# The last two chunks' output sums by Strassen in 128x256 products, behind all of h, with w_out's sums built by VectorE

## The chip, the cores and the metric

One core of a Trainium2 chip runs the whole program. The metric is the device time of one execution in microseconds (us). The runs shown are several executions of one program; the profile is of one more execution, with its own time beside it.

## The reference

Attention over 8 x 8 heads of 576 positions and 64 channels, with a window mask (half of the heads: the last 32 positions; the other half: every fourth of the last 128), gives x with 4608 tokens of 512 channels. A feed-forward block follows:

```python
scores = where(mask, 0.125 * q @ k.T, -1e9); attn = softmax(scores); x = attn @ v     # per head
h = x @ w_in                                    # 4608x512 by 512x2048
sp = np.maximum(h, 0.0) + np.log1p(np.exp(-np.abs(h)))        # softplus
g = h * erf(sp)
out = g @ w_out                                 # 4608x2048 by 2048x512
```

## The kernel before

Tokens go in nine chunks of 512 (`TOK`), d_ff in 16 blocks of 128 (`FT`), taken in 8 pairs (`SPC`, `PAIR`). Float32 values are kept as a high part, rounded to the type f32r, and a low part, so a product of two matrices is three TensorE products: high x high, high x low, low x high. Three chunks (`PAIRED`) are done plainly beside the attention. The other six form three pairs of chunks (`DOUBLES`), and h of a pair is computed by Strassen's scheme with seven products (`ORDER`, `mm1_big`): the two halves of the d_model contraction, the two blocks of a d_ff pair and the two chunks are the 2x2 blocks. A step d (0 to 23, 8 for each pair of chunks) has 7 x 6 = 42 products of 128x512. `take_big` adds the seven results into h of chunk A and chunk B of the pair; `load_left` fetches the left operands of step d + 2 from a DRAM buffer `ws` into one of two places in `win`.

Then `argument_big` makes softplus on ScalarE into `ls`, ScalarE makes erf of it in place, and `multiply_big` makes g = h * erf on VectorE. Chunk B's g goes to DRAM (`kept_g`), as its output sums come later; chunk A's is used at once.

The output sums (g @ w_out) are plain: an item is one pair of d_ff blocks of one chunk. `split_item` makes g's high and low part (`ghi` by ScalarE or VectorE, `glo` by VectorE), `products` are 2 x 4 x 3 = 24 products of 128x512 into four PSUM banks `acc`. `store` copies the four banks out when a chunk is done.

The order is written out by hand, and each engine runs its instructions in that order. `period(i)` runs item i of `ITEMS` in quarters of six products, and where `BIG` has i, the 42 products of a step of h in groups between the quarters. Steps 0 to 7 of h are in periods 0 to 7, steps 8 to 15 in 16 to 23, steps 16 to 23 in 32 to 39; the other periods have an item alone. There are 50 items; the last 16 are chunk 7 (A16 to A23) and chunk 8 (B16 to B23). In a period stand, in this order: the split of the item's second half; the first products of h and their takes; a quarter; products 2 and 3; erf of the step before; a quarter; `multiply_big` of A; the split of the next item's first half; products 4 and 5 with A's softplus; `multiply_big` of B; a quarter; product 6 with B's softplus; a quarter; transfers. `AFT` holds further jobs by period and quarter, above all the sums of the right operands of the next pair of chunks. The step's products alternate between two PSUM banks (`h` and `bank`, which is tile `tx`): product n waits until product n - 2 is taken. All loads and nearly all stores are issued by SyncE's queue (SP), in order.

PSUM has eight banks: `h`, `tx`, two for the attention (`sp`), four `acc`.

Of the kernel before, what the change touches and what calls it, by code (L numbers as in the profile page):

```python
# [29 lines left out]
DM, DF = 512, 2048  # L30
# [3 lines left out]
TOK = 512  # L34
NCH = NTOK // TOK
# [104 lines left out]
def attn_moe_kernel(ctx: ExitStack, tc: tile.TileContext, qk, v, masks, eye, w_in, w_out, out):  # L140
# [467 lines left out]
    def split(item, e, copy=None):  # L608
        ghi, glo = (work.tile([P, TOK], F32R, name=n) for n in ("ghi", "glo"))
        gs[item].append((ghi, glo))  # L610
        (copy or nc.vector.tensor_copy)(out=ghi, in_=e)  # L611
        nc.vector.tensor_tensor(out=glo, in0=e, in1=ghi.bitcast(F32), op=ALU.subtract)  # L612
# [22 lines left out]
    def mm(args):  # L635
        nc.tensor.matmul(args["out"], args["lhsT"], args["rhs"], start=args["start"], stop=args["stop"])  # L636
# [22 lines left out]
    def store(c):  # L659
        last = c == NCH - 1  # L660
        for tt in range(TOK // P):
            if c == 0:
                o = added[tt]
                nc.vector.tensor_tensor(out=o, in0=acc[tt], in1=o, op=ALU.add)
            else:
                if tt == 0 and c < PAIRED - 1:
                    o = doubles(2).bitcast(F32).rearrange("p n w -> p (n w)")[:, 0:DM]
                elif tt == 0:
                    o = small.tile([P, DM], F32, name="o", bufs=1)
                else:  # L670
                    o = io.tile([P, DM], F32, name="w", bufs=4)
                copy_for(tt)(out=o, in_=acc[tt])
            r = c * TOK + tt * P
            (nc.scalar if last and tt % 2 else nc.sync).dma_start(out=out[r:r + P, :], in_=o)
# [43 lines left out]
    def room_w():  # L718
        return [io.tile([P, TOK], F32, name="w", bufs=4) for _ in range(2)]
# [25 lines left out]
    for k in range(1, DOUBLES):  # L745
# [6 lines left out]
                    (i - 3, 3): [LESS["T4"], LO["T1"], HI["T4"], HI["B22"]],  # L752
                    (i - 2, 3): [LO["T4"], LO["B21"]], (i - 1, 3): [LO["B22"]]})

    def jobs(todo):
        for job, *args in todo:
            job(*args)

    ITEMS = [NT - 2, NT - 1] + [(kind_, i * SPC + k) for i in range(DOUBLES) for kind_ in "AB" for k in range(SPC)]

    def mm1_big(d, k):
        bank_ = (h, bank)[(7 * d + k) % 2]
        name = ORDER[k]
        w = left(NT + d).rearrange("p (b i c n) -> p b i c n", b=len(LEFT), i=2, c=2)[:, LEFT.index(name)]
        x = big[RIGHT[LEFT.index(name)]]
        for c in range(2):
            for n, (wi, xi) in enumerate(((0, 0), (0, 1), (1, 0))):
                nc.tensor.matmul(bank_, w[:, wi, c, :], x[c][:, xi, :],  # L768
                                 start=(c == 0 and n == 0), stop=(c == 1 and n == 2))

    def take_big(d, k):
        y = (h, bank)[(7 * d + k) % 2]
        if k == 0:
            hs["A", d], hs["B", d] = pair_of(d)
        a, b = hs["A", d], hs["B", d]
        add = lambda out, to: nc.vector.tensor_tensor(out=out, in0=y, in1=to, op=ALU.add)  # L776
        if k == 0:
            nc.vector.tensor_copy(out=a[:, 1], in_=y)  # L778
        elif k == 1:
            add(a[:, 0], a[:, 1])  # L780
        elif k == 2:
            add(b[:, 0], a[:, 1])
        elif k == 3:
            add(b[:, 1], b[:, 0])
        elif k == 4:
            add(a[:, 1], b[:, 1])
        elif k == 5:
            nc.vector.tensor_tensor(out=b, in0=y.rearrange("p (j n) -> p j n", j=1).broadcast_to([P, PAIR, TOK]),
                                    in1=b, op=ALU.add)
        else:  # L790
            add(b[:, 0], b[:, 0])

    def pair_of(d):
        if d % 2:
            return [work.tile([P, PAIR, TOK], F32, name="hc") for _ in range(2)]
        return [slab(i) for i in range(2)]

    def argument_big(kind_, d):
        if (kind_, d) in hs:
            ls[kind_, d] = work.tile([P, PAIR, TOK], F32, name="s")  # L800
            nc.scalar.activation(out=ls[kind_, d], in_=hs[kind_, d], func=AF.Softplus)  # L801

    def multiply_big(kind_, d):
        e = hs[kind_, d]
        nc.vector.tensor_tensor(out=e, in0=e, in1=ls[kind_, d], op=ALU.mult)
        gs[kind_, d] = []
        if kind_ == "B":
            nc.sync.dma_start(out=kept_g[d // SPC][d % SPC], in_=e)

    def load_g(item):  # L810
        kind_, d = item
        if kind_ == "B":
            e = work.tile([P, PAIR, TOK], F32, name="hc") if d % 4 > 1 else slab(1 - d % 4)
            nc.sync.dma_start(out=e, in_=kept_g[d // SPC][d % SPC])
            hs[item] = e

    def split_item(item, j):
# [3 lines left out]
    def item_products(item):  # L821
        if isinstance(item, int):
            _, ftp, run = STEPS[item]
            first, last = ftp == RUNS[run][1], ends(item)
        else:
            ftp = item[1] % SPC
            first, last = ftp == 0, ftp == SPC - 1
        for j in range(PAIR):
            yield from products(item, ftp * PAIR + j, j, first and j == 0, last and j == PAIR - 1)

    def done(item):
        if isinstance(item, int):
# [87 lines left out]
            finish(m)  # L920

    pending = []

    with tc.manual_schedule():
        nc.gpsimd.memset(idle, 1.0)
# [199 lines left out]
```

## Time and profile before

| what | us |
|---|---|
| median of 3 runs (892.6 to 894.48) | 892.87 |
| the profiled execution | 892.89 |
| its span, first to last instruction | 890.9 |
| TensorE busy in the span | 871.2 |
| VectorE busy | 633.6 |
| ScalarE busy | 564.5 |
| GpSimd busy | 81.3 |

The span is what the profile's rows add up to; the execution's own time is 2 us longer. Engines: PE is TensorE's products, PEld its weight loads, DVE VectorE, ACT ScalarE, POOL GpSimd, SP SyncE. A product's duration in a row includes its way through the array, so two that follow each other overlap; the pitch (start to start) is what a product costs in a stream. "L636" is line 636 of the kernel. In a row of a group stand line, engine, operation, output and inputs by the program's names, shapes and count, then busy us, mean ns of one, and idle time of the engine before them with what ended it.

### The profile page before, as it was taken

To read this page: it belongs to the slowest core of one execution; us is meant where nothing else is said; L and a number is where in the kernel's file an instruction comes from. 1 tells how busy PE (TensorE), PEld (TensorE's weight loads), DVE (VectorE), ACT (ScalarE), POOL (GpSimd) and SP (SyncE) were. 2 spreads that over 40 slices of the span, in tenths; PEclk is the share of its full clock that TensorE was granted. 3 is DMA by queue.
4 is the path that set the end of the run, shared out by engine and by line. 5 is a ranking of instruction groups with operands and counts; after the bars stand their busy time and mean duration, and the time that the engine had idled before them with its cause. 6 is when DMAs were issued, how large, how long until landed. Compare 5 with 4: busy or idle time off the path is not lost.

```text
span 890.9 us, 20870 instructions
## 1 busy us (share of the span) xinstructions
PE 871.2 (98%) x8134; PEld 700.1 (79%) x8134; DVE 633.6 (71%) x1575; ACT 564.5 (63%) x1271; POOL 81.3 (9%) x97
## 2 busy tenths in 40 slices
PE   7799999999999999999999999999999999999998
PEld 3367888888888888788887778888888888888886
DVE  5878888987798889777676765666566647576622
ACT  6889888897788886675677442774445434445321
POOL 2312201111111110011000000010000000000000
PEclk9999999999999999999999999999999999999999
DMA  8874446464658896566675741674449125442341
GB/s 272 295 245 154 128 155 197 148 232 127 222 203 270 295 341 248 172 224 221 204 239 200 272 176 54 209 237 161 166 155 361 51 83 200 166 154 83 140 144 48
DMA packets 66915, 170.41 MB, mean 191 GB/s; under 512 B 7680, under 2 KB 14592, under 8 KB 63744
## 3 DMA queue, kind: packets, MB, share of 16 engines
q1 hardware_dynamic: 66528, 168.55, 55.1%
q8 instruction: 64, 1.05, 0.5%
q10 hardware_dynamic: 288, 0.52, 0.2%
q14 instruction: 35, 0.29, 0.1%
HBM read 122.91 MB, written 46.14 MB: 190 GB/s over the span
## 4 chain that ended last, share of the span: by engine, by line
PE 91%; DVE 5%; DMA 1%; ACT 1%; issue 1%; POOL 1%; SPq 0%; DVEq 0%; POOLq 0%; ACTq 0%
PE acc L636 43%; PE h L768 13%; PE tx L768 13%; PE h L521 7%; PE tx L521 7%; PE sp L275 3%; PE sp L217 3%; PE sp L256 1%; PE h L357 1%; DMA qk<-in_qk_dram 1%; DMA v<-in_v_dram 1%; DVE w L458 0%; DVE w L459 0%; DVE prob L228 0%; DVE win L453 0%
## 5 line engine op out<-in xcount | busy, mean ns | idle before, releaser
L636 PE MATMUL acc<-wout_hi,ghi 128*128 128x512 f32 x576 | 227.4, 395 | 0.5 <-DVE ghi L611 0.4
L636 PE MATMUL acc<-wout_lo,ghi 128*128 128x512 f32 x576 | 224.6, 390 | 0.0
L636 PE MATMUL acc<-wout_hi,glo 128*128 128x512 f32 x576 | 159.0, 389 | 0.0
L636 PEld LDWEIGHTS acc<-wout_hi,ghi 128*128 128x128 f32 x576 | 108.2, 188 | 23.3 <-DVE ghi L611 0.9
L636 PEld LDWEIGHTS acc<-wout_hi,glo 128*128 128x128 f32 x576 | 108.1, 188 | 22.8
L636 PEld LDWEIGHTS acc<-wout_lo,ghi 128*128 128x128 f32 x576 | 108.2, 188 | 21.7
L251 POOL TENSOR_TENSOR prob<-prob,rinv 128x256 f32<-128x256 f32 x72 | 72.7, 1016 | 477.0 <-DVE ssum L249 239.9
L238 ACT ACTIVATE prob<-prob,nmax 128x64 f32<-128x64 f32 x288 | 96.3, 338 | 10.5 <-DVE nmax L228 10.3
L801 ACT ACT_TABLE_LOAD x24 | 30.8, 1283 | 93.0 <-DVE dbl L776 47.3
L768 PE MATMUL tx<-win 128*128 128x512 f32 x288 | 74.1, 392 | 0.8 <-DVE hc L778 0.8
L228 DVE CUSTOM_DVE_ANT_0 prob<-sp,cst 128x64 f32<-128x64 f32 x288 | 45.3, 220 | 40.6 <-ACT rows L317 28.2
L768 PE MATMUL h<-win 128*128 128x512 f32 x288 | 74.0, 392 | 0.0
L768 PEld LDWEIGHTS tx<-win 128*128 128x128 f32 x288 | 53.5, 188 | 12.7 <-DVE hc L778 1.2
L768 PEld LDWEIGHTS h<-win 128*128 128x128 f32 x288 | 53.4, 188 | 12.0 <-DVE dbl L778 0.8
L612 DVE TENSOR_TENSOR glo<-hc,ghi 128x512 fp32r<-128x512 f32 x50 | 34.5, 692 | 33.4 <-PE acc L636 22.6
L238 ACT ACTIVATION_READ_ACCUMULATOR prob<-prob,nmax 128x1 f32 x288 | 54.7, 190 | 0.0
L612 DVE TENSOR_TENSOR glo<-dbl,ghi 128x512 fp32r<-128x512 f32 x48 | 33.4, 696 | 28.3 <-PE acc L636 15.6
L521 PE MATMUL h<-x,win 128*128 128x512 f32 x192 | 48.8, 396 | 0.0
L877 ACT ACTIVATE s<-s 128x1024 f32<-128x1024 f32 x48 | 48.2, 1052 | 0.3
L521 PE MATMUL tx<-x,win 128*128 128x512 f32 x192 | 48.0, 392 | 0.0
L801 ACT ACTIVATE s<-hc 128x1024 f32<-128x1024 f32 x24 | 25.5, 1061 | 34.9 <-DVE hc L776 22.8
L611 ACT CAST ghi<-hc 128x512 fp32r<-128x512 f32 x24 | 14.9, 623 | 50.0 <-PE acc L636 41.9
(146 smaller groups left out, 1519.7 us busy)
## 6 DMA issues: line engine op xcount, KB each, us to landing
win<-ws SPq DMA_DIRECT2D x24, 1024.0 KB, 5.0
v<-in_v_dram SPq DMA_DIRECT2D x72, 256.0 KB, 4.9
win<-ws SPq DMA_DIRECT2D x24, 768.0 KB, 5.1
qk<-in_qk_dram SPq DMA_DIRECT2D x48, 272.0 KB, 4.8
dbl<-in_w_in_dram SPq DMA_DIRECT2D x16, 512.0 KB, 4.4
dbl<-in_w_out_dram SPq DMA_DIRECT2D x16, 512.0 KB, 3.9
ws<-x SPq DMA_DIRECT2D x32, 256.0 KB, 4.3
qk<-in_qk_dram SPq DMA_DIRECT2D x24, 288.0 KB, 4.3
```

The costliest lines, as they stand in the source:

```text
L217: nc.tensor.matmul(sps[h][r * STRIP:(r + 1) * STRIP, i, p, :], qkz[i][hs, s * STRIP:(s + 1) * STRIP], qkz[i][hs, at:at + KEYS], start=True ...
L228: nc.vector.tensor_tensor_reduce(out=pr[:, g, :], in0=sps[h][:, u % 2, p, :], in1=mask[QUADS.index(kinds(u, p))], scale=-SCALE, scalar=HUG ...
L238: nc.scalar.activation(out=probs[u][:, j, :], in_=probs[u][:, j, :], func=AF.Exp, scale=-1.0, bias=nmax[:, j:j + 1], accum_out=sums[u][:, ...
L251: nc.gpsimd.tensor_tensor(probs[u], probs[u], rinv.broadcast_to([P, 2 * PARTS, KEYS]), op=ALU.mult)
L275: nc.tensor.matmul(xp[h * D:(h + 1) * D, qs], vt[ks, s, h, :], pt[ks, h * P + s * STRIP:h * P + (s + 1) * STRIP], start=True, stop=True, t ...
L521: nc.tensor.matmul((h, bank)[j], win_at[:, ftp, j, cc // 2, w, cc % 2, :], x[cc], start=(k == 0 and i == 0), stop=(k == CC - 1 and i == 2))
L611: (copy or nc.vector.tensor_copy)(out=ghi, in_=e)
L612: nc.vector.tensor_tensor(out=glo, in0=e, in1=ghi.bitcast(F32), op=ALU.subtract)
L636: nc.tensor.matmul(args["out"], args["lhsT"], args["rhs"], start=args["start"], stop=args["stop"])
L768: nc.tensor.matmul(bank_, w[:, wi, c, :], x[c][:, xi, :], start=(c == 0 and n == 0), stop=(c == 1 and n == 2))
L801: nc.scalar.activation(out=ls[kind_, d], in_=hs[kind_, d], func=AF.Softplus)
L877: nc.scalar.activation(out=e, in_=e, func=AF.Erf)
```

## The change

- `ITEMS` ends before the last two items of chunk 6 (`REST`: B14 and B15). Periods run only to 31, so they hold no step of h of the last pair.
- `final(d)` runs the eight steps 16 to 23 of h, with no output sums between. The products rotate over four banks (`bank_of`: h, tx and the two `sp`), product 0 is copied by ScalarE and no longer by VectorE, and both chunks' g go to `kept_g`. In program order: product 0 and its take, erf of the step before, product 1, `multiply_big` of A, products 2 and 3, `multiply_big` of B, product 4 with A's softplus, products 5 and 6 with B's softplus, then jobs of a table `LATE`.
- `rest_steps` runs `REST` plainly (48 products of 128x512), and then stores chunk 6.
- The output sums of chunks 7 and 8 run by Strassen. A step s (16 in all: `LASTS`) takes one chunk, one half of its tokens (256) and two pairs of d_ff blocks; token halves of 128, the d_ff halves and the halves of 256 output columns are the 2x2 blocks. Seven products of 2 x 3 TensorE products of 128x256 each: 42. Each of the seven accumulates over four steps in its own bank, and the banks (all eight, `bank_at`) shift by one every four steps. `sums_out` adds the seven into four output blocks after every fourth step.
- VectorE makes the left operands' sums from g (`row_sums`, 4 jobs of 256 elements a partition a step) and the low parts (`operands`), ScalarE the high parts; this runs two steps ahead. g is loaded again from `kept_g` (`load_e`).
- The right operands need sums of w_out. For each of eight parts p, three jobs build them: `sub_whole` (2 VectorE adds of 512), `sub_sums` (4 of 256 and 2 ScalarE casts), `sub_split` (2 VectorE of 512, 4 stores of 256 KB to `wd`). The table `SUBS` puts p = 0 into periods 9, 11, 13, p = 1 to 4 into periods 20 to 23, p = 5 into 25, 27, 29, p = 6 into 31; `LATE` has the rest. They are loaded again (1 MB for each p) into the places in `win` that h's operands leave (`load_sums`).

```diff
-    kept_g = [dram.tile([SPC, P, PAIR, TOK], F32, name=f"g{i}") for i in range(DOUBLES)]
+    kept_g = {("B", i): dram.tile([SPC, P, PAIR, TOK], F32, name=f"g{i}") for i in range(DOUBLES)}
+    kept_g["A", FIN] = dram.tile([SPC, P, PAIR, TOK], F32, name="ga")
...
+    SUBS = [lambda p: sub_whole(p), lambda p: sub_sums(p), lambda p: sub_split(p)]
+    for p, places in enumerate([((9, 0), (11, 0), (13, 0))] + [((i, 0), (i, 1), (i, 3)) for i in range(20, 24)] +
+                               [((25, 0), (27, 0), (29, 0)), ((31, 0), (31, 3))]):
...
-    ITEMS = [NT - 2, NT - 1] + [(kind_, i * SPC + k) for i in range(DOUBLES) for kind_ in "AB" for k in range(SPC)]
+    ITEMS = [NT - 2, NT - 1] + [(kind_, i * SPC + k) for i in range(FIN) for kind_ in "AB" for k in range(SPC)]
+    ITEMS, REST = ITEMS[:-2], ITEMS[-2:]
+    def bank_of(d, k):
+        return (h, bank, *spb)[(7 * d + k) % (4 if d >= FIN * SPC else 2)]
...
         if k == 0:
-            nc.vector.tensor_copy(out=a[:, 1], in_=y)
+            (nc.scalar.copy if d >= FIN * SPC else nc.vector.tensor_copy)(out=a[:, 1], in_=y)
...
+    def sums_product(s, k):
+        q = s % QUART
+        y, (xh, xl) = bank_at(s, k), operand(s, k)
+        for j in range(2):
+            at_, (wh, wl) = slice(j * P, (j + 1) * P), right(2 * q + j)[k]
+            for n, (x, w) in enumerate(((xh, wh), (xh, wl), (xl, wh))):
+                nc.tensor.matmul(y, x[:, at_], w, start=(q == 0 and j == 0 and n == 0),
+                                 stop=(q == QUART - 1 and j == 1 and n == 2))
...
+    def final(d):
+        for k in (0, 1):
+            mm1_big(d, k)
+            take_big(d, k)
+            if k == 0 and d > FIN * SPC:
+                for kind_ in "AB":
+                    e = ls[kind_, d - 1]
+                    nc.scalar.activation(out=e, in_=e, func=AF.Erf)
+        if d > FIN * SPC:
+            multiply_big("A", d - 1)
+        for k in (2, 3):
+            mm1_big(d, k)
+            take_big(d, k)
+        if d > FIN * SPC:
+            multiply_big("B", d - 1)
+        load_left(NT + d + 2, 0)
+        mm1_big(d, 4)
+        take_big(d, 4)
+        argument_big("A", d)
+        for k in (5, 6):
+            mm1_big(d, k)
+            take_big(d, k)
+        argument_big("B", d)
+        load_left(NT + d + 2, 1)
+        jobs(LATE.get(d - FIN * SPC, ()))
...
+    LATE = {0: [(sub_split, 6)], 1: [(sub_whole, 7)], 2: [(sub_sums, 7), (load_e, 0, room_halves)],
+            3: [(sub_split, 7)], 4: [(row_sums, 0, room_w)], 5: [(operands, 0, 0), (operands, 0, 1)],
+            6: [(operands, 0, 2), (operands, 0, 3), (load_rest,), (load_sums, 0), (load_sums, 1)],
+            7: [(split_rest, 0, 0), (load_e, 1, lambda: slab(1)), (load_sums, 2), (load_sums, 3)]}
+    def rest_steps():
+        d = DOUBLES * SPC - 1
+        for n, item in enumerate(REST):
+            todo_ = item_products(item)
+            def quarter():
+                for _, args in zip(range(6), todo_):
+                    mm(args)
+            if n == 0:
+                split_rest(0, 1)
+            quarter()
+            if n == 0:
+                for kind_ in "AB":
+                    nc.scalar.activation(out=ls[kind_, d], in_=ls[kind_, d], func=AF.Erf)
+            else:
+                row_sums(1, room_s)
+            quarter()
+            if n == 0:
+                split_rest(1, 0)
+                multiply_big("A", d)
+            quarter()
+            if n == 0:
+                multiply_big("B", d)
+            quarter()
...
+        store(done(REST[-1]))
+        load_sums(6)
+        load_sums(7)
+    def sums_step(s):
+        last_ = s % QUART == QUART - 1
+        for g, ks in enumerate(GROUPS):
+            for k in ks:
+                sums_product(s, k)
+            if s == 0 and g == 0:
+                operands_all(1)
+            if g == 0:
+                row_sums(s + 2, room_s)
+            if last_:
+                for k in ks:
+                    sums_out(s, k)
+            operands(s + 2, g)
+        load_e(s + 4, lambda: room_e(s + 4))
...
+        for d in range(FIN * SPC, DOUBLES * SPC):
+            final(d)
+        rest_steps()
+        for s in range(len(LASTS)):
+            sums_step(s)
```

More of the change, by code (lines that the diff above doesn't have):

```diff
@@ L771, in take_big @@
     def take_big(d, k):
-        y = (h, bank)[(7 * d + k) % 2]
+        y = bank_of(d, k)
         if k == 0:
@@ L922, in attn_moe_kernel, with less, sub_room @@
     pending = []
+    wd = dram.tile([SPC, P, 2, 2, TOK], F32, name="wd")
+    subs, wider = {}, {}
+    def less(out, a, b, op=ALU.subtract):
+        nc.vector.tensor_tensor(out=out, in0=a, in1=b, op=op)
+    def sub_room(p):
+        if p == 0:
+            r, hi = (work.tile([P, PAIR, TOK], F32, name="s") for _ in range(2))
+            return [r[:, j] for j in range(2)], [hi.bitcast(F32R)[:, j] for j in range(2)]
+        r = [work.tile([P, S], F32, name="rows", bufs=4)[:, 0:TOK] for _ in range(2)]
+        return r, [one.tile([P, QW + KW if p % 2 else TOK], F32R, name=f"{('v', 'qk')[p % 2]}{j}")[:, 0:TOK]
+                   for j in range(2)]
@@ new lines, in sub_whole, with sub_sums @@
+    def sub_whole(p):
+        subs[p] = sub_room(p)
+        for j, r in enumerate(subs[p][0]):
+            less(r, wout_hi[:, 2 * p + j, :].bitcast(F32), wout_lo[:, 2 * p + j, :].bitcast(F32), ALU.add)
+    def sub_sums(p):
+        (b11, b12), (b21, b22) = [(t[:, 0:HN], t[:, HN:TOK]) for t in subs[p][0]]
+        less(b11, b12, b11)
+        less(b12, b22, b12)
+        less(b22, b22, b11)
+        less(b21, b22, b21)
+        for r, hi in zip(*subs[p]):
+            nc.scalar.copy(out=hi, in_=r)
@@ new lines, in right, with load_e @@
+    def right(p):
+        w11, w12, w21, w22 = ([w[:, 2 * p + j, n * HN:(n + 1) * HN] for w in (wout_hi, wout_lo)]
+                              for j in range(2) for n in range(2))
+        return w11, w21, sum_at(p, 1, 1), sum_at(p, 0, 1), sum_at(p, 0, 0), w22, sum_at(p, 1, 0)
+    es, rs, ops = {}, {}, {}
+    GROUPS = ((0, 1), (2, 3), (4, 5), (6,))
+    def load_e(s, room):
+        if s < len(LASTS):
+            kind_, half, q = LASTS[s]
+            es[s] = room()
+            for k in range(2):
+                to = es[s][k] if isinstance(es[s], list) else es[s][:, k].rearrange("p (j n) -> p j n", j=PAIR)
+                nc.sync.dma_start(out=to,
+                                  in_=kept_g[kind_, FIN][2 * q + k][:, :, half * HN:(half + 1) * HN])
@@ new lines, in row_sums @@
+    def row_sums(s, room):
+        if s < len(LASTS):
+            r = rs[s] = room()
+            for ks, e in parts_of(s):
+                a11, a12, a21, a22 = (e[:, :, j, n, :] for n in range(2) for j in range(PAIR))
+                s2, s3, s1, s4 = (t.rearrange("p (n k m) -> p n k m", n=2, k=2)[:, n, ks]
+                                  for t in r for n in range(2))
+                less(s1, a21, a22, ALU.add)
+                less(s2, s1, a11)
+                less(s3, a11, a21)
+                less(s4, a12, s2)
@@ new lines, in room_s, with op_room @@
+    def room_s():
+        t = work.tile([P, PAIR, TOK], F32, name="s")
+        return [t[:, 0], t[:, 1]]
+    def op_room(s):
+        if s % 2 == 0:
+            return [work.tile([P, S], F32R, name="rows", bufs=4)[:, 0:TOK] for _ in range(4)] + [
+                one.tile([P, QW + KW], F32R, name=f"qk{i}")[:, 0:TOK] for i in range(2)] + [
+                one.tile([P, TOK], F32R, name="v0")]
+        return [work.tile([P, TOK], F32R, name=n) for n in ("ghi", "glo", "ghi", "glo")] + [
+            one.tile([P, TOK], F32R, name="v1"), one.tile([P, TOK], F32R, name="pT1"),
+            small.tile([P, DM], F32R, name="o", bufs=1)]
@@ new lines, in operands @@
+    def operands(s, g):
+        if s >= len(LASTS):
+            return
+        if g == 0:
+            ops[s] = op_room(s)
+        room = ops[s]
+        if g == 3:
+            hi, lo = room[6][:, 0:HN], room[6][:, HN:TOK]
+            at_ = lambda t, ks: t.rearrange("p (k n) -> p k n", k=2)[:, ks]
+            src = [(ks, e[:, :, 1, 1, :]) for ks, e in parts_of(s)]
+        elif g:
+            hi, lo = room[2 * g:2 * g + 2]
+            at_ = lambda t, ks: t
+            src = [(None, rs[s][g - 1])]
+        else:
+            hi, lo = room[0:2]
+            at_ = lambda t, ks: t.rearrange("p (j k n) -> p j k n", j=PAIR, k=2)[:, :, ks]
+            src = [(ks, e[:, :, :, 0, :].rearrange("p k j n -> p j k n")) for ks, e in parts_of(s)]
+        for ks, t in src:
+            nc.scalar.copy(out=at_(hi, ks), in_=t)
+        for ks, t in src:
+            less(at_(lo, ks), t, at_(hi, ks).bitcast(F32))
```

98 lines of the change are left out of this document (93 added, 5 removed).

## The prediction

> **What bounds the kernel now.** I read first the page's span, busy times and clock, then the chain, then the windows of the stretches that the change touches, then the groups of instructions and a few stretches of the timeline.
>
> ```profile
> span 890.9 us, 20870 instructions
> PE 871.2 (98%) x8134; PEld 700.1 (79%) x8134; DVE 633.6 (71%) x1575; ACT 564.5 (63%) x1271; POOL 81.3 (9%) x97
> PEclk9999999999999999999999999999999999999999
> PE 91%; DVE 5%; DMA 1%; ACT 1%; issue 1%; POOL 1%; SPq 0%; DVEq 0%; POOLq 0%; ACTq 0%
> ```
>
> TensorE is the chain (91%) at full granted clock; VectorE and ScalarE have room on average. The windows say where. Columns: stretch, length, busy time and count of PE, PEld, DVE, ACT, POOL, clock, DMA share, GB/s.
>
> ```profile
> 620.70:669.60 48.90, 48.90 (x217) 40.50 (x216) 32.47 (x43) 22.62 (x21) 0.00 (x0) 1.00 0.45 158
> 675.00:680.50 5.50, 5.50 (x25) 4.53 (x25) 4.29 (x7) 1.21 (x2) 0.00 (x0) 1.00 1.05 382
> 713.10:832.80 119.70, 119.70 (x529) 99.10 (x529) 75.73 (x102) 51.60 (x49) 0.00 (x0) 1.00 0.38 132
> 832.80:887.40 54.60, 54.58 (x241) 44.86 (x239) 18.94 (x27) 15.73 (x23) 0.00 (x0) 1.00 0.32 110
> ```
>
> From 713.1 to 832.8 the last eight steps of h (42 products each) run interleaved with eight items of plain sums (24 products each); from 832.8 to 887.4 ten items of plain sums run alone. TensorE never waits: 54.6 us / 241 = 0.2266 us a product of 128x512. The 768 products from 713.1 to 887.4 take 174.1 us, all of it on the path. This is the stretch that the change rewrites.
>
> **The products.** Of the 18 items two stay plain (48 products) and 16 become 16 steps of 7 x 2 x 3 = 42 products of 128x256. At 128x512 stay 336 + 48 = 384: 87.0 us. New are 672 of 128x256. No row shows this shape, so I bound it. Weight loads first:
>
> ```profile
> L636 PEld LDWEIGHTS acc<-wout_hi,ghi 128*128 128x128 f32 x576 | 108.2, 188 | 23.3 <-DVE ghi L611 0.9 <-ACT ghi L611 0.8
> L275 PEld LDWEIGHTS sp<-pT,v 64*64 64x64 f32 x1824 | 29.3, 134 | 10.6 <-DVE s L605 4.6 <-issue 2.8 <-DVE dbl L805 1.1
> L217 PEld LDWEIGHTS sp<-qk 64*32 64x32 f32 x2304 | 24.1, 106 | 7.2 <-issue 5.4 <-DVE w L459 0.3 <-DVE w L457 0.2
> 303.79 0.19 PEld L636 LDWEIGHTS acc<-wout_hi,ghi 128*128 128x128 f32 x1
> 303.89 0.19 PEld L636 LDWEIGHTS acc<-wout_lo,ghi 128*128 128x128 f32 x1
> 7.07 0.74 PEld L357 LDWEIGHTS <-plain 128*128 128x128 bf16 x4
> L357 PEld LDWEIGHTS <-plain 128*128 128x128 bf16 x70 | 5.2, 105 | 6.5 <-issue 2.4 <-POOL plain L925 1.3
> ```
>
> A load of 128 columns lasts 188 ns, but 32, 64 and 128 columns (106, 134, 188) make it 0.85 ns a column on a fixed 79, and two such loads start 0.10 to 0.11 us apart at 303.79, after short products. So a load holds the array for about 0.110 us, the floor of the new pitch; 0.188 (126 us for all) is excluded by that pair of rows. Upper bound: four bf16 loads within 0.74 us give (0.74 - 0.105) / 3 = 0.212 us for a product of the same 512 columns, against 0.2266 here. The 0.014 us come either with each product (0.106 + 0.014 = 0.120) or with the columns (0.113). I take 0.117, the middle of these two, since no row tells them apart: 78.6 us. Saved: 174.1 - 87.0 - 78.6 = 8.5 us; 13.2 at the floor, 6.5 at 0.120.
>
> The Trainium skill (TensorE: Matmul & The Clock Gate, Back-to-back issue gap) gives N / 2.4 + 2.5 ns, 109 ns here; the bf16 rows come near it (0.212 for 512 columns, where it gives 0.216), the f32r rows lie above (0.2266). By it the saving would be 13.7 us.
>
> **What is taken from under the products.** Before, a step of h lasts 42 + 24 products, 14.96 us. After, `final` runs eight steps with nothing between: 42 x 0.2266 = 9.52 us each. VectorE and ScalarE hand data to each other in program order, and within `final(d)` this order closes a loop: softplus of A needs the sum of product 4; softplus of A and B, then ScalarE's copy of the next step's product 0, then the erf table and erf; `multiply_big("A")` stands before the takes of products 2 and 3, `multiply_big("B")` before that of product 4. Prices:
>
> ```profile
> 753.89 1.28 ACT L801 ACT_TABLE_LOAD   x1 [5.86 <-DVE dbl L776]
> 755.18 1.06 ACT L801 ACTIVATE s<-dbl 128x1024 f32<-128x1024 f32 x1
> 758.73 1.28 ACT L877 ACT_TABLE_LOAD   x1
> 760.02 2.01 ACT L877 ACTIVATE s<-s 128x1024 f32<-128x1024 f32 x2
> L593 ACT COPY hc<-h 128x512 f32<-128x512 f32 x8 | 4.5, 566 | 0.0
> L260 ACT COPY pT<-acc 128x256 f32<-128x256 f32 x7 | 2.6, 366 | 0.0
> L611 ACT CAST ghi<-hc 128x512 fp32r<-128x512 f32 x24 | 14.9, 623 | 50.0 <-PE acc L636 41.9 <-DMA hc<-g 6.7 <-issue 1.4
> 752.52 0.69 DVE L612 TENSOR_TENSOR glo<-hc,ghi 128x512 fp32r<-128x512 f32 x1
> 753.13 0.68 DVE L776 TENSOR_TENSOR dbl<-h,dbl 128x512 f32<-128x512 f32 x1
> 754.14 1.23 DVE L788 TENSOR_TENSOR dbl<-tx,dbl 128x1024 f32<-128x1024 f32 x1 [0.33 <-PE tx L768]
> 755.28 1.22 DVE L805 TENSOR_TENSOR hc<-hc,s 128x1024 f32<-128x1024 f32 x1
> 327.44 0.42 DVE L540 TENSOR_TENSOR plain<-plain 128x256 f32<-128x256 f32 x1
> 327.90 0.42 DVE L541 TENSOR_TENSOR plain<-plain 128x256 f32<-128x256 f32 x1
> ```
>
> The table load waits for VectorE's sum (row 1: 5.86 us on `dbl`, and it starts 0.08 after 753.81), so it is in the loop. Independent VectorE jobs follow at 0.61 (128x512) and 1.14 (128x1024), dependent ones 0.04 after the end. The loop: 0.08 + 1.29 softplus table + 2.01 softplus A, B + 0.57 copy + 0.02 + 1.29 erf table + 1.06 erf A + 0.05 + 1.14 multiply A + 0.73 product 2 + 0.61 product 3 + 1.14 multiply B + 0.69 product 4 = 10.68 us, 1.16 more than TensorE needs. The fifth and sixth takes (1.14 + 0.73) lie beside the softplus.
>
> The Trainium skill (ScalarE: Activation LUTs, What ACT_TABLE_LOAD costs) charges 2.66 us for a change of table, a drain included; the trace disagrees: 753.89 to 755.18 and 758.73 to 760.02 are 1.29 each. With 2.66 the sum would be some 20 us longer.
>
> `LATE` puts ScalarE work into the same loop, ahead of the next copy: behind d=18 two casts that wait for four VectorE sums (4 x 0.46 behind the takes; + 1.6 us), behind d=21 and d=22 the first operands (two pieces of 0.36 and one of 0.62, then one of 0.62 and two small: + 1.2 each). Together 4.0. VectorE's own `LATE` jobs (1.3 to 2.2 us) stand beside softplus B, copy, erf table and erf A (over 3 us free): nothing.
>
> The first step has no multiplies: its product 4 is added at 5 x 1.36 + 0.2 + 0.69 = 7.7 us. Seven loops (74.8) and 4.0 bring the same point of the last step to 86.5. The plain sums of the rest wait for 0.08 + 1.29 + 2.01 + the cast 0.62 + 0.05: 90.5 us. TensorE's own work in the eight steps is 76.2, so 14.3 us of idle TensorE, partly in the steps (four banks let it run four products ahead), partly before the rest.
>
> **Edits that I cost at little.** `SUBS` puts about 4.3 us of VectorE (2 + 2 jobs of 0.61, four of 0.46) and two casts into each of periods 20 to 23: VectorE 32.47 of 48.9 us becomes about 13.9 of 14.96 a period, and it catches up at each period's wait for TensorE; behind period 23 some 0.5 us stick out. The bound is 0 to 3 us with the short items at 9 to 13 and 25 to 31. I take 0.5. Uncovered it would be 30 us. The sums are written (32 stores of 256 KB) outside the full stretch at 675.0 (382 GB/s, share 1.05); those stores wait on SyncE for VectorE's splits and hold only transfers due a period later.
>
> In the sums VectorE has per step four row sums (4 x 0.46) and four splits (3 x 0.61 + 0.34, which is 0.42 less the overlap of 0.08): 4.0 us, and 2.9 us of results every fourth step, 4.7 in all against 42 x 0.117 = 4.9. Operands are made two steps ahead, so nothing is charged. SyncE loads 2 MB of w_out sums during the end of `final`, 2 MB at its end, 2 in the rest and 2 behind chunk 6's stores; these last and three loads of operands, 6 MB in some 18 us, make 333 GB/s, under the 382 shown. Charged nothing. Uncovered, each late MB is about 3 us.
>
> The end changes little: one subtraction of 128x256 (0.42) in place of this copy, then one store.
>
> ```profile
> 887.42 0.59 ACT L672 COPY w<-acc 128x512 f32<-128x512 f32 x1 [0.77 <-PE acc L636]
> out_dram<-w ACTq DMA_DIRECT2D x2, 256.0 KB, 2.1
> ```
>
> **The sum.** The profiled execution took 892.89 us around its span of 890.9; the median of the runs, 892.87, is the same. -8.5 + 14.3 + 0.5 - 0.2 = +6.1: 899.0 us. The saving of the products is real and smaller than the wait that the bare steps of h open.
>
> **The rivals.**
> - *The loop hides* (faster). If VectorE and ScalarE close the loop within 9.52 us, by 1.2 us less than my rows, TensorE waits only for the last step: 0.2 + 0.69 + softplus B 1.06 + cast 0.62 + 0.13 = 2.7 us, and the sum is -8.5 + 2.7 + 0.5 - 0.2 = -5.5: 887.4. For it: four banks in place of two, and busy times of 7 us an engine a step, well under 9.52. Against: the order above. It decides at a loop of 9.52; every 0.1 is 0.7 us. Chance 0.2.
> - *The products run at the load's floor*, 0.110: -13.2 + 14.3 + 0.5 - 0.2 = +1.4, 894.3, within what can be told from no change. For it: the pair at 303.79. Chance 0.18. (The Trainium skill's gap of TensorE: Matmul & The Clock Gate, Back-to-back issue gap, would give this rival 893.8; the pair at 303.79 does not contradict it.)
> - *VectorE bounds the sums.* If each job there waits for the one before (0.73 and 0.46), a step is 1.84 + 2.19 + 0.46 and 0.8 of results, 5.3 us against 4.9, in 14 steps 5.6 us: 904.6. Late transfers of w_out's sums would look alike, 3 us a MB. Chance 0.12.
> - My forecast, 0.5.
>
> Differences under 0.2% (1.8 us) can't be told from no change. Faster: the first rival and a part of the second, 0.24; same 0.18; slower 0.58. The range takes in the faster rival's end and the third: 888 to 907; for the likeliest case alone 895 to 904.
>
> **What would show it.** Right: TensorE gaps of about 1.2 us a step in `final` from the third step on, ended by VectorE's takes, and one of some 4 to 6 us before the first plain product of the rest, ended by ScalarE's cast; a pitch of 0.113 to 0.120 of the 128x256 products with no gaps; VectorE 90% busy there. Wrong: a gapless `final`; a pitch at 0.110 or above 0.125; gaps between the 16 steps, ended by DMA or VectorE; gaps in periods 20 to 31 over 3 us.

## The result, and the profile after

| kernel | median us | runs | ratio to before, 95% interval |
|---|---|---|---|
| before | 893.62 (892.6 to 895.57) | 5 | |
| after | 922.08 (920.22 to 922.39) | 5 | 1.0309 [1.029, 1.0328] |

The change costs 28.5 us. The forecast was 899.0 us with a range up to 907: the sign was right, the size missed by 23 us. The profiled execution of after took 922.39 us around a span of 920.6, 29.7 us more than before's span. One execution among the experiments below was five times longer than its fellows and is left out of the times.

Page of after: span, busy times, granted clock by slice, and the shares of the chain that ended last.

```profile
span 920.6 us, 21964 instructions
PE 876.4 (95%) x8422; PEld 712.5 (77%) x8422; DVE 697.5 (76%) x1747; ACT 600.9 (65%) x1347; POOL 80.5 (9%) x97
PEclk9799999999999999999999999999999999987999
PE 78%; DVE 8%; ACT 5%; DMA 5%; issue 3%; SPq 1%; POOL 0%; DVEq 0%; ACTq 0%; POOLq 0%
```

TensorE held 91% of before's chain and holds 78% of this one; VectorE, ScalarE and transfers have the rest. The windows of after from period 20 on show where (columns as in the prediction: stretch, length, PE, PEld, DVE, ACT, POOL, clock, DMA share, GB/s):

```profile
615.00:720.60 105.60, 101.49 (x437) 80.91 (x436) 85.73 (x137) 49.36 (x64) 0.00 (x0) 1.00 0.61 204
720.60:805.30 84.70, 78.46 (x337) 62.19 (x335) 58.87 (x83) 53.98 (x59) 0.00 (x0) 1.00 0.72 252
805.30:810.40 5.10, 0.35 (x3) 0.01 (x1) 3.10 (x5) 3.85 (x5) 0.00 (x0) 0.80 1.00 357
810.40:823.70 13.30, 13.30 (x49) 10.77 (x50) 7.47 (x12) 5.58 (x7) 0.00 (x0) 0.82 0.72 230
823.70:833.00 9.30, 9.30 (x79) 9.27 (x77) 2.07 (x4) 2.14 (x4) 0.00 (x0) 1.00 0.63 230
833.00:843.00 10.00, 0.20 (x3) 0.02 (x1) 0.04 (x1) 0.48 (x2) 0.00 (x0) 0.63 0.94 324
843.00:852.10 9.10, 8.68 (x49) 8.38 (x50) 8.96 (x26) 4.66 (x11) 0.00 (x0) 0.65 0.88 338
852.10:917.50 65.40, 65.40 (x548) 65.32 (x546) 52.49 (x121) 26.44 (x51) 0.00 (x0) 1.00 0.34 108
```

The second row is `final`, the third the wait before the rest, the fourth the rest, the others the Strassen sums. The first product of each stage gives the account of the span (start of `final` 713.1 us before, 720.6 after):

| stage | by its own work, us | measured | difference |
|---|---|---|---|
| periods up to the start of h's last eight steps | 713.1 (before) | 720.6 | +7.5 |
| `final` and the wait behind it | 336 x 0.2266 = 76.1 | 89.8 | +13.6 |
| the rest | 48 x 0.2266 = 10.9 | 13.3 | +2.4 |
| Strassen sums | 672 x 0.120 = 80.6, 6.5 less than the 384 products replaced | 93.8 | +13.2 - 6.5 |
| end | 3.5 (before) | 3.1 | -0.4 |

The sum is +29.8, against 29.7 in the spans. Three quarters of the sums' excess (10.0 of 13.2 us) is one hole: from 833 to 843 TensorE, VectorE and ScalarE all but stand still and transfers run (324 GB/s). The waits of after from 822 to 846, ScalarE's timeline at their end, and SyncE's from 804 on say why:

```profile
ACT o L1070 <- DMA out_dram<-o: 16.5, 1, 16.5
PEld acc L1093 <- ACT o L1070: 10.0, 1, 10.0
842.52 0.40 ACT L1070 CAST o<-dbl 128x256 fp32r<-128x256 f32 x1 [16.51 <-DMA out_dram<-o]
805.89 0.32 SPq L827 DMA_DIRECT2D g<-dbl  x1
814.34 1.18 SPq L1006 DMA_DIRECT2D dbl<-ga  x2
815.61 2.22 SPq L986 DMA_DIRECT2D win<-wd  x4
817.93 1.59 SPq L827 DMA_DIRECT2D ga<-hc  x1
819.57 0.65 SPq L827 DMA_DIRECT2D g<-hc  x1
829.57 1.19 SPq L1006 DMA_DIRECT2D hc<-ga  x2
830.85 2.65 SPq L986 DMA_DIRECT2D win<-wd  x4
833.59 1.70 SPq L679 DMA_DIRECT2D out_dram<-o  x1
```

Read from the top: TensorE waits 10.0 us for ScalarE's cast of an operand of step 1, which is to be written into tile `o`. Tile `o` is also the first output block of chunk 6, and the cast waits 16.5 us for that block's store. The store is issued only at 833.59 and has landed at 842.5, behind 2 MB of w_out's sums issued from 830.85. It is issued so late because SyncE's queue stood still twice before: the load of g for step 1 (into `dbl`, 814.34) waited for the store of the g that lay there (issued 805.89), and the load for step 2 (into `hc`, 829.57) for the store issued at 819.57:

```profile
SPq L1006 <- DMA g<-hc: 9.3, 1, 9.3
SPq L1006 <- DMA g<-dbl: 8.1, 1, 8.1
```

Such a store of 512 KB lands after 3.0 us in the median of this kernel, and here after 8.4 and 10.0 us: 2 to 3 MB of other loads were issued just before it. In periods 20 to 31 the products' starts show nine gaps, 6.6 us in all with the slower product behind each (a gap is what lies between two starts beyond the product's own pitch; the window's busy time counts a product's way through the array, so its idle share of 4.1 us is smaller). The waits of after from 615 to 712:

```profile
ACT qk L973 <- DVE rows L949: 10.9, 6, 4.1
ACT v L973 <- DVE rows L949: 10.5, 4, 6.0
ACT ghi L616 <- DMA dbl<-g: 5.2, 1, 5.2
PEld acc L641 <- ACT ghi L616: 3.8, 3, 2.0
```

ScalarE's two casts of a w_out sum (L973, into `v` and `qk`) wait 21.4 us for VectorE's four additions, and what stands behind them in ScalarE's queue waits with them: the cast of g's high part (L616), for which TensorE waits. One such cast waits 5.2 us for a load of g, which shares the queue with the four stores of part p = 4.

### The profile page after: what moved, and what is told of

Read it like the earlier page. It is cut to its first block, busy times and chain, and to the rows that moved or that the text cites. A ratio compares the mean times of both kernels' runs of the same rounds, so it can differ in the third digit from the quotient of the medians.

```text
span 920.6 us, 21964 instructions
## 1 busy us (share of the span) xinstructions
PE 876.4 (95%) x8422; PEld 712.5 (77%) x8422; DVE 697.5 (76%) x1747; ACT 600.9 (65%) x1347; POOL 80.5 (9%) x97
## 4 chain that ended last, share of the span: by engine, by line
PE 78%; DVE 8%; ACT 5%; DMA 5%; issue 3%; SPq 1%; POOL 0%; DVEq 0%; ACTq 0%; POOLq 0%
PE acc L641 28%; PE tx L787 8%; PE h L787 8%; PE h L526 7%; PE tx L526 7%; PE acc L1093 4%; PE sp L280 3%; PE sp L222 3%; PE sp L1093 3%; PE sp L787 2%; PE sp L261 1%; PE tx L1093 1%; PE h L1093 1%; DMA out_dram<-w 1%; DVE hc L795 1%
## 5 line engine op out<-in xcount | busy, mean ns | idle before, releaser
L641 PE MATMUL acc<-wout_hi,ghi 128*128 128x512 f32 x448 | 179.4, 400 | 8.5 <-ACT ghi L616 7.2
L641 PE MATMUL acc<-wout_lo,ghi 128*128 128x512 f32 x448 | 175.8, 392 | 0.0
L641 PE MATMUL acc<-wout_hi,glo 128*128 128x512 f32 x448 | 124.4, 391 | 0.0
L641 PEld LDWEIGHTS acc<-wout_hi,ghi 128*128 128x128 f32 x448 | 84.7, 189 | 28.7 <-ACT ghi L616 9.1
L641 PEld LDWEIGHTS acc<-wout_lo,ghi 128*128 128x128 f32 x448 | 84.8, 189 | 16.7
L322 ACT COPY rows<-sp 128x128 f32<-128x128 f32 (+7 forms) x167 | 27.6, 308 | 28.2 <-PE sp L222 27.7
L526 PEld LDWEIGHTS h<-x,win 128*128 128x128 f32 x192 | 35.4, 188 | 8.0
L820 ACT ACTIVATE s<-dbl 128x1024 f32<-128x1024 f32 x24 | 25.1, 1059 | 25.3 <-DVE dbl L795 25.2
L526 PEld LDWEIGHTS tx<-x,win 128*128 128x128 f32 x192 | 35.7, 188 | 7.5
L280 PEld LDWEIGHTS sp<-pT,v 64*64 64x64 f32 x1824 | 29.3, 134 | 10.6 <-DVE s L610 4.6
```

The lines of the kernel that those rows point to most:

```text
L280: nc.tensor.matmul(xp[h * D:(h + 1) * D, qs], vt[ks, s, h, :], pt[ks, h * P + s * STRIP:h * P + (s + 1) * STRIP], start=True, stop=True, t ...
L322: nc.scalar.copy(out=to, in_=src)
L526: nc.tensor.matmul((h, bank)[j], win_at[:, ftp, j, cc // 2, w, cc % 2, :], x[cc], start=(k == 0 and i == 0), stop=(k == CC - 1 and i == 2))
```

## The experiments

All are edits of the kernel after unless another base is named; each time stands against runs of the kernel before on the same chip.

**An output block of its own for the store.** Chunk 6's first block is copied into a `w` tile like the others, so no operand waits for its store.

```diff
-                elif tt == 0:
+                elif tt == 0 and c != NCH - 3:
```

> One edit: chunk 6's first output block goes through tile w instead of tile o, which the operands of step 1 need. Theory A (the 10.1 us gap at 832.9 is only the tile: step 1's cast into o waits for chunk 6's store, which SyncE issues at 833.6): the gap goes, and with it the 2 us of halved clock behind it, about 910 us. Rival B (SyncE's queue and the bulk loads are late as a whole; without the tile the next wait is g of step 2, landed at 834.7, and the w_out sums 4 and 5, landed at 841.8): gaps of 3 to 4 us each remain at steps 2, about 916 to 919 us.

Measured: 919.34 us (918.72 to 920.61), ratio 1.0292 [1.0258, 1.0325], not told apart from after's. The hole of 10 us is gone, and in its place stand several of 0.2 to 2.6 us between 832 and 856. Of the waits from 822 to 860:

```profile
DVE s L949 <- DMA dbl<-ga: 9.3, 1, 9.3
DVE s L949 <- DMA hc<-ga: 6.7, 1, 6.7
PEld sp L1093 <- DMA win<-wd: 3.6, 2, 2.6
```

Now VectorE waits for g itself (`dbl`, `hc`) and TensorE for w_out's sums (`win`). SyncE's queue still waits 8.1 and 9.2 us for the two stores of g. The shared tile was only the last link; the transfers as a whole are late. The low clock behind the gaps lasts longer than in after: 44 products of 128x256 stand about 0.213 us apart, against 22 behind the one hole.

**SyncE's order.** The round trips are taken out as well: g of steps 1 and 2 is loaded into idle tiles (`slab(2)` and `plain`) at the end of `final`, before the big loads; g of step 4 goes to the rest; sums 2 to 5 are issued together, and chunk 6's store stands behind sums 6 and 7.

```diff
-            7: [(split_rest, 0, 0), (load_e, 1, lambda: slab(1)), (load_sums, 2), (load_sums, 3)]}
+            7: [(split_rest, 0, 0), (load_e, 1, lambda: slab(2)), (load_e, 2, room_plain)] +
+               [(load_sums, p) for p in range(2, 6)]}
...
-        store(done(REST[-1]))
         load_sums(6)
         load_sums(7)
+        store(done(REST[-1]))
```

> On top of the tile edit of e1_out_tile: g of the sums' steps 1 and 2 is loaded into two tiles that nothing is stored from (dbl2 and plain, free after h's product 4), the w_out sums 2 to 5 right behind them at the end of final, sums 6 and 7 and g of step 4 ahead of chunk 6's store. No load then waits for a store's landing. Theory (round trips on SyncE's queue: 9.3 us at 820 to 829.6 for g of step 2, 8.1 for step 1): the 10.1 us gap and what e1_out_tile had in its place go, at most 2 us of gaps stay in the 16 steps, about 908 us. Rival (the volume itself, some 12 MB from 800 to 850 us): 4 to 6 us of gaps stay at steps 2 to 4, about 914 us.

Measured: 908.10 us (907.04 to 909.79), ratio 1.0176 [1.0151, 1.0201]; against after's 1.0309 that is 1.33% or 11.9 us, and 14.3 in the spans. The window of the sums:

```profile
822.70:903.20 80.50, 80.50 (x673) 80.42 (x671) 64.27 (x150) 35.23 (x67) 0.00 (x0) 1.00 0.46 160
```

TensorE is never idle and at full clock; 80.5 us for 672 products is 0.120 each. The bytes are the same as in after, and SyncE's two waits for stores of g are gone. So neither VectorE nor the bandwidth bounds the sums; the order in one queue did. The edit takes out the waits and also issues sums 4 and 5 earlier (from 809 us, in after from 831); what each is worth alone was not tried.

**No building of w_out's sums.** Leaves out the jobs of parts 0 to 6 (additions, casts and stores); their loads take the last part's bytes instead.

```diff
-            also(i, q, (sub, p))
+            pass
```

> Leaves out the building of w_out's sums for p = 0 to 6 (VectorE jobs, casts and stores in the periods 9 to 31 and the first of LATE); all loads stay, from the sums of p = 7. If these jobs cause the 6.6 us of TensorE gaps between 622 and 702 us (before: none there), these go: 915 us. Rival: the gaps come from other loads of the change in these periods (both chunks' g, items cut short): they stay, 921 us.

Measured: 912.94 us (912.03 to 913.81), ratio 1.0218 [1.0185, 1.0251], that is 0.91% or 8.1 us under after's; the spans differ by 8.8. The window of periods 20 to 31:

```profile
615.00:712.10 97.10, 97.10 (x431) 80.38 (x430) 63.88 (x92) 42.70 (x52) 0.00 (x0) 1.00 0.47 168
```

Every gap there is gone. The building costs 8 to 9 us as it is placed, not 0.5.

**The additions on GpSimd.** Parts 0 to 5 are added and split by GpSimd, with the jobs spread over more quarters.

```diff
+    def by(p):
+        return nc.gpsimd if p < 6 else nc.vector
...
-        less(b11, b12, b11)
+        less(b11, b12, b11, eng=by(p))
```

> w_out's sums for p = 0 to 5 are added and split by GpSimd instead of VectorE, the casts half a period later, the stores one period later and those of p = 4 behind the full stretch of loads (period 28). If VectorE's and ScalarE's share of these jobs is the cause of the 6.6 us of gaps, 916 us. Rival: GpSimd slows VectorE where both read the memory, or holds ScalarE's casts longer: no gain or a loss, 921 to 926 us.

Measured: 922.66 us (922.36 to 923.91), ratio 1.033 [1.0297, 1.0363]: nothing gained. In periods 20 to 31 the nine gaps become one of 0.4 us and one of 2.4 at 678, with a lower clock behind it. What that saves is lost earlier, where GpSimd builds part 0: from 500 to 524 us TensorE's gaps are 4.0 us, and 0.6 in after. VectorE, GpSimd and TensorE in this run behind the gap at 678:

```profile
680.22 0.43 DVE L616 CAST ghi<-hc 128x512 fp32r<-128x512 f32 x1
680.75 0.69 DVE L617 TENSOR_TENSOR glo<-hc,ghi 128x512 fp32r<-128x512 f32 x1
681.96 3.17 POOL L952 TENSOR_TENSOR rows<-wout_hi,wout_lo 128x512 f32<-128x512 f32 x2 [3.37 <-DMA wd<-rows]
682.50 1.50 DVE L616 CAST ghi<-hc 128x512 fp32r<-128x512 f32 x1
684.10 1.58 DVE L617 TENSOR_TENSOR glo<-hc,ghi 128x512 fp32r<-128x512 f32 x1
682.01 0.63 PE L641 MATMUL acc<-wout_lo,ghi 128*128 128x512 f32 x1
682.44 0.63 PE L641 MATMUL acc<-wout_hi,ghi 128*128 128x512 f32 x1
```

The cast takes 0.43 us before GpSimd begins and 1.50 beside it, the subtraction 0.69 and 1.58: beside GpSimd's additions VectorE's own jobs stretch.

**The multiplies later in `final`.** On after: `multiply_big` of A behind the take of product 3, of B behind product 4 and A's softplus; this takes both out of the loop.

```diff
-        if d > FIN * SPC:
-            multiply_big("A", d - 1)
         for k in (2, 3):
             mm1_big(d, k)
             take_big(d, k)
         if d > FIN * SPC:
-            multiply_big("B", d - 1)
+            multiply_big("A", d - 1)
         load_left(NT + d + 2, 0)
         mm1_big(d, 4)
         take_big(d, 4)
         argument_big("A", d)
+        if d > FIN * SPC:
+            multiply_big("B", d - 1)
```

> One edit: in final(d) the two multiplies of step d-1 stand behind the takes of products 3 and 4, not ahead of products 2 and 4's takes. By the loop of the prediction (10.7 us a step) the loop becomes about 8.9 us, under TensorE's 9.5: TensorE's 7.5 us of gaps in final fall to under 2, and the 5 us before the rest to about 3; alone this gives 914 us. Rival: what follows hangs on SyncE's queue, not on TensorE, so the gap before step 1's last product grows by what final gains and the total stays at 919 to 922 us.

Measured: 924.16 us (920.34 to 924.59), ratio 1.0345 [1.0307, 1.0384]: no gain. The gaps within `final` fell from 7.5 to 5.5 us, and the hole in the sums grew from 10.0 to 12.1. VectorE's waits within `final`:

```profile
DVE hc L795 <- DMA g<-hc: 4.4, 2, 3.3
DVE dbl L795 <- DMA g<-dbl: 4.0, 2, 2.2
```

With g ready later its stores start later, and the takes that reuse these tiles wait for their landing. The same edit on the kernel with SyncE's order mended, with `load_left` moved behind the multiplies:

```diff
-        load_left(NT + d + 2, 0)
         mm1_big(d, 4)
         take_big(d, 4)
         argument_big("A", d)
+        if d > FIN * SPC:
+            multiply_big("B", d - 1)
+        load_left(NT + d + 2, 0)
```

> e6_queue, and in final the multiplies of the step before behind the takes of products 3 and 4 (as e3_late_multiplies), but with both stores of g ahead of the left operands on SyncE's queue (in e3 a take waited 2.2 and 3.3 us for B's store, which stood behind a load of 1 MB). Loop theory: gaps in final from 7.5 to 2 to 3 us (LATE's casts), before the rest from 4.9 to about 4: 901 to 903 us. Rival (the wait only moves to the stores' landing): gaps of 5 us stay in final, 905 to 907 us.

Measured: 902.0 us (901.54 to 902.20), ratio 1.0104 [1.008, 1.0129], 0.72% or 6.4 us under the base. TensorE's longest waits for operands from 719 to 804 now are these:

```profile
PEld acc L641 <- ACT ghi L616: 5.0, 1, 5.0
PEld sp L787 <- ACT hc L797: 2.0, 1, 2.0
PEld sp L787 <- ACT dbl L797: 0.6, 1, 0.6
```

Some 2.3 us are left within the eight steps, most of it ended by ScalarE's copy (L797), and the 5.0 before the rest. With the queue out of the way the loop is what the prediction took it for, and the place of the multiplies is its lever. The load of `load_left` moved with them, so that it no longer stands ahead of B's store; its own share was not tried.

**Two other orders in `final`**, on the kernel with SyncE's order mended, both with the multiplies later. In the first, product 0 of the next step is taken before `LATE`'s jobs, which stand behind the erfs, and the rest's first split is in step 0:

```diff
+            for kind_ in "AB":
+                e = ls[kind_, d - 1]
+                nc.scalar.activation(out=e, in_=e, func=AF.Erf)
+            jobs(LATE.get(d - 1 - FIN * SPC, ()))
...
+        if d + 1 < DOUBLES * SPC:
+            product(d + 1, 0)
```

> e6_queue, and final in another order: multiply A behind the take of product 3, multiply B behind that of 4, the next step's product 0 ahead of softplus B, LATE's jobs behind the erfs; and the first item of the rest is loaded and split during final. By the loop of rows: table and two softplus 3.4, erf table and erf A 2.4, multiply A, product 4, multiply B, 5 and 6 below 9.5 us a step; with the casts of LATE some 2 us of gaps stay in final and none before the rest (12.6 before, and 2.4 of halved clock behind): 894 to 896 us. Rival (final is not held by this order but by LATE's casts or the loads of the left operands): gaps of 6 us or more stay in final, over 900 us.

Measured: 915.02 us (911.95 to 917.12), ratio 1.0249 [1.0218, 1.0279], slower than its base. VectorE's waits from 719 to 826:

```profile
DVE glo L617 <- ACT ghi L616: 6.6, 2, 4.9
DVE hc L795 <- DMA g<-hc: 5.5, 2, 3.0
DVE dbl L795 <- DMA g<-dbl: 5.4, 2, 2.7
DVE qk L949 <- ACT qk L1070: 5.3, 1, 5.3
DVE rows L949 <- ACT rows L1070: 4.8, 1, 4.8
```

The subtractions that follow a cast of `LATE` stand in VectorE's queue ahead of the takes, and these casts now come behind two erfs. The two longest gaps within `final`, 2.1 us at 736 and 3.5 at 792, end with takes that stood behind such a subtraction: the loop got longer by another member. But the takes also wait 10.9 us for stores of g to land, as where the multiplies moved alone, since `load_left` stands ahead of B's store again; the two causes were not separated. The second adds to this the GpSimd additions for all parts:

```diff
-        less(b11, b12, b11)
+        less(b11, b12, b11, eng=nc.gpsimd)
```

> e7_queue_final, and w_out's sums on GpSimd (all eight parts, stores of a part one period later, part 4's behind the full stretch of loads). If VectorE's share of these jobs, the casts that wait for them in ScalarE's queue and the late g behind the stores are the 6.6 us of gaps at 622 to 702 us, at most 1.5 us of them stay: 889 to 891 us, 3 us under the kernel before. Rival as in e5_sums_on_gpsimd, where one gap of 2.6 us took the place of nine: 893 to 896 us.

Measured: 922.73 us (920.35 to 924.88), ratio 1.0337 [1.0309, 1.0365]: worse still, with a gap of 4.4 us at 741 and one of 2.6 at 680.

**The rest's first item early.** On the kernel with queue and multiplies mended: the first item's g is loaded and split in step 0 of `final`, so that no cast stands behind the last softplus; the last step's erfs come a quarter later; the loads of g and of sums 2 to 5 move behind the rest's first quarter; and a part's casts become a job of their own.

```diff
+    LATE = {0: [(sub_split, 6), (split_rest, 0, 0), (split_rest, 0, 1)], 1: [(sub_whole, 7)],
...
+                load_e(1, lambda: slab(2))
+                load_e(2, room_plain)
+                for p in range(2, 6):
+                    load_sums(p)
```

> e9_queue_late_multiplies, with the first plain item of the rest loaded ahead of final and split behind its first step, and the casts of w_out's sums of p = 7 one step later than their sums. The wait of 4.9 us before the rest, and the 2.3 us of halved clock behind it, go: 895 to 897 us. Rival (what the early casts cost ScalarE comes back as gaps in final, as in e7_queue_final): 900 us or more.

Measured: 900.34 us (897.97 to 901.51), ratio 1.0083 [1.0056, 1.011]. In the profiled span of 896.2 the wait before the rest is gone: `final` with what lies behind it went from 83.6 to 77.1 us, the rest from 13.2 to 12.5. New are gaps of 1.4 us in the rest and of 1.9 in the sums, the latter with a low clock behind it, and the sums went from 80.5 to 84.4. So less was gained than removed (4.0 in the spans, 1.7 in the medians; the intervals of the ratios overlap).

**The sums' jobs spread.** On that one: part 1 in periods 12 to 15, parts 2 to 4 one job a quarter in periods 20 to 22, none in 23, part 5 in periods 28 and 29; additions, casts and splits never in the same quarter.

```diff
-    for p, places in enumerate([((9, 0), (11, 0), (11, 0), (13, 0))] +
-                               [((i, 0), (i, 1), (i, 1), (i, 3)) for i in range(20, 24)] +
+    for p, places in enumerate([((9, 0), (10, 0), (10, 3), (12, 0)), ((12, 3), (14, 0), (14, 3), (15, 0))] +
+                               [((i, 0), (i, 1), (i, 2), (i, 3)) for i in range(20, 23)] +
```

> e10_first_rest_early, with w_out's sums kept on VectorE but moved: p = 1 from period 20 to 12 to 15, none in 23 to 27, p = 5 and 6 in 28 to 31, and the casts behind the erfs of a period. If the 6.6 us of gaps come from the places (period 23 to 27, where loads run at their limit and the periods are short), at most 2.5 us of them stay: 890 to 892 us, level with the kernel before or just under it. Rival (any place costs the same): 895 us or more.

Measured: 893.77 us (892.52 to 898.17, 10 runs), ratio 1.0025 [1.0009, 1.004], 6.6 us under its base in the same batch. Of the 8 to 9 us that the building cost, most is gone with all of the work still done, on the same engines: what periods 20 to 31 take beyond their products fell from 6.5 to 2.0 us in the profiled executions. The edit both spreads the jobs and takes part 1 out of these periods; the two were not tried apart.

**Earlier sums, later stores.** On that one: sums 2 and 3 are loaded within `final`, the last g's stores and multiplies move behind the rest's first item, the sums' results get tiles of their own, g of step 5 is loaded ahead, and parts 2 and 3 overlap in periods 20 to 22.

```diff
+        if d == DOUBLES * SPC - 1:
+            load_sums(2)
+            load_sums(3)
...
+        load_e(5, lambda: one.tile([P, 2, S], F32, name="x2")[:, :, 0:TOK])
+        for kind_ in "AB":
+            keep(kind_, d)
```

> e11_sums_spread with four waits of its trace taken away by order alone: w_out sums 2 and 3 loaded as soon as h's last products 0 and 1 are through, sums 6 and 7 and g of step 5 ahead of the last stores of g and chunk 6's output, the sums' results in tiles of x instead of w, both splits of the rest's second item ahead of the last erfs, and the sums of p = 2 and 3 a quarter of a period later. In e11 these places cost TensorE 2.0 + 1.4 + 0.3 us in the sums (sums 7 landed at 822.0, first used at 820; results waited for w), 1.5 us in the rest and 0.8 us in periods 20 and 21: 6 us. Theory (what is left are waits, not products): 887 to 889 us, faster than the kernel before by 0.4%. Rival (the volume of transfers from 786 to 826 us, 350 GB/s, is the bound and the waits move): 891 to 893 us.

Measured: 895.70 us (891.36 to 898.67, 12 runs), ratio 1.0034 [1.0021, 1.0048]: not the gain expected. VectorE's waits from 795 to 815:

```profile
DVE s L954 <- DMA dbl<-ga: 4.4, 1, 4.4
```

g of step 1 landed at 808.7 behind sums 2 and 3, and row sums that waited for it held chunk 6's copies: 3.1 us of TensorE at 807.9. In the periods the overlapped parts opened gaps of 1.5, 0.8 and 0.9 us. Both were put back and the rest kept:

```diff
-        if d == DOUBLES * SPC - 1:
-            load_sums(2)
-            load_sums(3)
...
-                load_sums(4)
-                load_sums(5)
+                for p in range(2, 6):
+                    load_sums(p)
```

> e12_order with two of its edits undone: w_out sums 2 and 3 again behind g of steps 1 and 2 (in e12 g of step 1 landed at 808.7 behind them, and chunk 6's copies stood behind its row sums: 3.1 us), and the building of sums 2 to 4 as in e11_sums_spread (in e12 one gap of 1.7 us at 651.9 and two of about 0.8 us at 676 and 688 came in). Theory (each gap has its own place and goes with it): at most 3 us of gaps behind 610 us, 888 to 890 us, 0.3% under the kernel before. Rival (the volume bounds the sums' start, and the wait moves once more): 892 us or more.

Measured: 890.59 us (888.39 to 892.28, 7 runs) against 893.12, ratio 0.9969 [0.9956, 0.9981]: 0.3% faster than before. From 615 us on no single wait of TensorE for an operand is longer than 0.9 us. The window of the sums:

```profile
806.30:887.40 81.10, 80.80 (x673) 80.48 (x671) 66.19 (x155) 34.16 (x67) 0.00 (x0) 1.00 0.55 200
```

## Why the prediction was wrong, step by step

- **The step that failed: the transfers of the sums, "charged nothing".** The prediction compared volume with bandwidth (333 GB/s needed, 382 shown), and the volume did fit: in the kernel with SyncE's order mended the same bytes move with no gap. What it left out is that SyncE issues in order and that some of its loads must wait for a store of the same tile to land. Two such round trips stopped the issue of all later transfers for 8.1 and 9.3 us, and the store of tile `o`, which an operand needs, came at the end of that row. It cost the hole of 10.0 us, 1.2 in smaller ones and the low clock behind. The mended order gave 11.9 us back by the ratios. The prediction named late transfers only as a remark to its third rival, at 3 us a MB; the price is a round trip behind other loads and not one of bytes.
- **`SUBS` was mis-sized: 0.5 us, bound 3; it cost 7.5 in the span, and 8 to 9 were gained without it.** The prediction summed VectorE's busy time against the period, and VectorE did have the room: 85.73 of 105.6 us are busy (the prediction's own terms make 14.2 us a period of 14.96, not the 13.9 that it wrote). It asked who sticks out at the end of period 23, and not who is queued behind the casts on ScalarE; these wait 21.4 us for VectorE, ahead of the cast that TensorE needs. It also said that the stores lie outside the full stretch at 675.0, which is wrong for part 4: its stores are issued from 675.0 to 677.1 with other loads behind them, the load of g comes at 684.4 and not at 676.9 as in before, and ScalarE's cast of that g, for which TensorE waits, stands still for 5.2 us. The same jobs, spread and in part moved to earlier periods, took 6.6 us back.
- **The idle TensorE of `final`, the largest term, was right.** Forecast 14.3 us and the rest's start 90.5 us behind the first product; measured 13.6 and 89.8. The steps have eight gaps of 0.4 to 1.4 us, most of them ended by VectorE's takes, and the wait before the rest is 5.1 us, ended by ScalarE's cast, as written. The loop is seen in VectorE's multiplies (L824), which stand ahead of takes and wait 11.0 us for ScalarE's erf. Waits from 720 to 811:

```profile
DVE dbl L824 <- ACT s L1139: 6.1, 4, 1.7
DVE hc L824 <- ACT s L1139: 4.9, 3, 1.7
PEld sp L787 <- DVE hc L795: 3.3, 2, 1.6
PEld acc L641 <- ACT ghi L616: 5.2, 1, 5.2
```

  So the rival in which the loop hides did not come true. That moving the multiplies opens the loop was shown only with the queue mended (6.4 us, `load_left` moved as well); in after itself the queue takes their place.
- **The products were mis-sized by 2.0 us.** Their pitch is 0.120, the upper of the two values between which 0.117 was the middle: the 0.014 us above the bf16 rows belong to each product and not to its columns. Saved: 6.5 us, not 8.5. The rival at the load's floor, 0.110, falls.
- **Not in the sum at all: the clock behind a long wait.** The 5.1 us before the rest and the 10.0 in the sums cost twice. In the rest the first products of after stand 0.427 us apart, nearly twice 0.2266:

```profile
810.99 0.63 PE L641 MATMUL acc<-wout_lo,ghi 128*128 128x512 f32 x1
811.41 0.63 PE L641 MATMUL acc<-wout_hi,ghi 128*128 128x512 f32 x1
811.84 0.63 PE L641 MATMUL acc<-wout_lo,ghi 128*128 128x512 f32 x1
```

  This is the 2.4 us by which the rest is longer, with a granted clock of 0.82 in its window; some 1.9 us behind the hole in the sums are of the same kind (22 products of 128x256 about 0.213 us apart, granted clock 0.65). The Trainium skill (TensorE: Matmul & The Clock Gate, Part 1: The HAM clock gate) says that the array falls to half its clock after about 3.4 us idle and recovers after as much sustained work; 512 columns at half of 2.4 GHz are 0.427 us, and the trace agrees. On the idle time it does not: the gap of 2.4 us at 678 in the run with GpSimd's additions was followed by the same pitch, and so was every gap of 2.1 us or more behind 560 us in the kernels run here. The prediction forecast a wait of 4 to 6 us and should have added this.

Two of the signs of being wrong that the prediction named came true: gaps of 6.6 us in periods 20 to 31, where it allowed 3, and a gap among the steps of the sums that goes back to a DMA. The terms as measured: +7.5 (forecast 0.5), +13.6 (14.3), +2.4 (0), -6.5 (-8.5), +13.2 (0), -0.4 (-0.2).

## What to carry to other kernels

Before bytes are set against bandwidth, walk an in-order DMA queue entry by entry and ask of each what it waits for; a load that waits for a store's landing stops everything behind it, and the store is as slow as the loads issued before it. A small job for an idle engine is priced by what stands behind it in that engine's and its partner's queue, and a busy share of 80% says nothing on that: the same jobs cost 8 us as first placed and little when spread and in part moved to earlier periods. A wait of TensorE of 2 us or more is priced with the half-clock stretch that can follow it (2.4 us behind 5.1 here); and where several waits lie behind one another, an edit that removes one shows nothing until those behind it are gone (the multiplies moved alone: nothing; with the queue mended: 6.4 us).

## What the runs showed that was not expected

- A product of 128x256 in f32r has a pitch of 0.120 us (80.50 us for 672 with no gap), and one of 128x512 0.2266. Halving the columns costs 6% in rate.
- A store of 512 KB, 3.0 us in the median, took 8.4 and 10.0 us behind loads of 2 to 3 MB, and one of 256 KB took 8.9.
- VectorE's 128x512 subtraction took up to 1.58 us beside GpSimd's additions and 0.69 without, its cast 1.50 and 0.43.
- With nearly all the waits gone the change is worth 0.3% (0.9969 [0.9956, 0.9981]): 5.9 us saved in the sums' window (81.1 against 87.0 for the products replaced), of which new jobs and small gaps leave less than half.
